# Attention blocks of the third and fourth chunk issued in pairs, with part of their transfers on ScalarE

## The chip, the cores and the metric

The kernel runs on one core of a Trainium2 chip. The metric is the device time of one execution in microseconds; the median of three runs is quoted, with the lowest and the highest.

## What is computed

A windowed attention over 8 batches and 8 heads of 576 positions with 64 columns each, then a feed-forward product over the 4608 tokens that it leaves. Heads 0 to 3 see the last 32 positions; heads 4 to 7 see every fourth of the last 128.

```python
scores = scale * np.matmul(q, k.transpose(0, 1, 3, 2))
rel = pos[:, None] - pos[None, :]
mask_plain = (rel >= 0) & (rel < window)                                          # window = 32
mask_dil = (rel >= 0) & (rel < window * dilation) & (rel % dilation == 0)         # dilation = 4
scores = np.where(masks[None], scores, -1e9)
attn = np.exp(scores - np.max(scores, axis=-1, keepdims=True))
attn = attn / (np.sum(attn, axis=-1, keepdims=True) + 1e-09)
x = np.matmul(attn, v)            # to 4608 tokens of 512
...
h = x @ w_in                      # 512 -> 2048
g = h * np.clip(h + 3.0, 0.0, 6.0) / 6.0
return g @ w_out                  # 2048 -> 512
```

All inputs and the output are fp32.

## The kernel before

**Products in three parts.** A matrix product of fp32 numbers is made of three products on TensorE: each operand is split into a high and a low part (`xh`, `xl`, `gh`, `gl`), and high by high, low by high and high by low are summed in PSUM.

**Tokens and steps.** The 4608 tokens lie in 12 chunks of 384. Chunks 0 to 3 are computed plainly, in steps `m` of one chunk and one block of 128 of the 2048 hidden columns, 16 steps a chunk: steps 32 to 47 are the third chunk, 48 to 63 the fourth. A step is `first(m)` and `second(m - 2)`. `first` is 12 matmuls of 128x384 into a bank of `ps_h` (L483 to L485), then relu on ScalarE (L491), the gate on VectorE (L494), which is the last to read the bank, and the two halves of the gated numbers, `gh` on ScalarE (L498) and `gl` on VectorE (L502). `second` is 9 matmuls of 128x512 into three banks of output (`ps_o`, L533 to L535). The other eight chunks follow with a Strassen scheme of fewer products (`pair`), streaming sums of weights from DRAM.

**PSUM.** Eight banks: two for `ps_h`, six for `ps_a`, of which three hold the output sums of a chunk.

**Attention.** The work is cut into 48 trios `t`. A block `block(ts, tv)` makes the scores of one trio and the values of an earlier one: 24 small matmuls of each kind on tiles of 64x32 of the array (L202, L220), by turns. The trace shows two records for each. Scores go through a chain: the mask is added (L228, VectorE; the reader of the bank), the largest taken (L239), subtracted (L243), the exponential (L249, ScalarE), two transposes by 32x32 blocks on VectorE (L325 into `a_t`, L326 into `a`), and four transfers of 24 KB (L331 to L335, function `cross`) that carry the pieces of `a_t` to the other partitions of `a`. `a` is what the value products of the block two later read. Values are normalised (L254 to L257, the last reader of their bank), transposed, crossed by four transfers in the same way (`xf`), then split into `xh` (L384, ScalarE) and a low part (L390 to L392, GpSimd) that the first product of later chunks reads. The loads of queries and keys (`kq`, L173) and of values (`v`, L182) for the trio two later are issued after the block.

The first 12 trios run with the first chunk, in an order written by hand. Blocks `b` = 0 to 17 (scores of trio 12 + b, values of trio 10 + b) run one by one among the steps of the third and fourth chunk, after `second`, about every 1.9 steps, at the steps that the list `spots` in the last function gives. Blocks from 18 on run inside `pair`.

**Order.** TensorE's instructions run in the order in which the steps are recorded. For VectorE, ScalarE, GpSimd and SyncE a planner sets the order: `op(engine, us, do, after, lag, takes, gives)` records an operation with an estimated duration, what it follows, a lag until its result has landed and the buffers that it takes and gives; `_in_time` lays the recorded operations out in time and gives each engine its list. All DMAs of the kernel before are issued by SyncE. All waits are on semaphores; a DMA also waits for the landing of the eighth DMA before it.

**Beside the blocks.** The same stretch prepares the weights for the Strassen part: sums of weight blocks on VectorE (L559, L567), a high part on ScalarE (L571), a low part (L576), and their stores to DRAM (`sums`, L583 to L590, on SyncE). At the end of a chunk the output is scaled and stored (`out`, L767).

## Time and profile before

| what | before |
|---|---|
| median of 3 runs | 870.23 us (867.68 to 871.71) |
| the profiled execution | 868.87 us |
| its span, first to last instruction | 867.1 us |
| granted TensorE clock, mean | 0.996 |
| DMA bytes moved | 148.30 MB, mean 171 GB/s |
| stretch of the single blocks | about 172 to 335 us |

Times in the profile are microseconds from the start of the span. PE is TensorE's matmul, PEld its weight load, DVE VectorE, ACT ScalarE, POOL GpSimd, SP SyncE; SPq is SyncE's issuing of DMAs. L202 is line 202 of the kernel. A row of a timeline gives start, duration, engine, line, operation, output <- inputs, shape and count, and in brackets the idle time before it with the event that ended it. A row of the windows gives the stretch, its length, then busy time and count of PE, PEld, DVE, ACT and POOL, the granted clock, the share of DMA and GB/s.

### The profile page before, as it was taken

The page shows a single profiled execution, that of the slowest core. Times are in us where ns is not written, and L with a number is a line of the kernel's source. Part 1 is how long each engine was busy: PE and PEld are TensorE (multiplying, and loading weights), DVE is VectorE, ACT ScalarE, POOL GpSimd, SP SyncE. Part 2 cuts the span into 40 slices and gives each one's busy share as a digit, 9 for nine tenths or more (in the row PEclk, how much of TensorE's full clock was granted, in tenths as well). Part 3 has the DMA queues.
Part 4 walks back from the last instruction along what each step waited for, and adds up shares of the span by engine and source line. Part 5 has one row for each costly group of instructions (what it writes and reads, how often), then busy time and mean ns, then how long its engine had stood idle before and what let it go on. Part 6 is the DMA issues. An engine that isn't in the chain of part 4 may idle for free.

```text
span 867.1 us, 20779 instructions
## 1 busy us (share of the span) xinstructions
PE 850.5 (98%) x8540; PEld 754.9 (87%) x8540; DVE 561.6 (65%) x1148; ACT 394.3 (45%) x746; POOL 30.9 (4%) x78
## 2 busy tenths in 40 slices
PE   7899999999999999999999999999999999999998
PEld 4698898888888878888888889888988889989997
DVE  3999986578886777665667565567556457343342
ACT  3788775343333424433436433335543335443334
POOL 0000000000100100100000000000000000000000
PEclk8999999999999999999999999999999999999999
DMA  8756335446677575664544655553654432753001
GB/s 288 278 163 205 122 122 173 155 158 214 206 230 230 150 254 181 208 219 146 210 145 147 224 173 178 180 187 114 226 193 145 145 120 95 277 193 113 1 1 73
DMA packets 83246, 148.30 MB, mean 171 GB/s; under 512 B 9808, under 2 KB 33360, under 8 KB 83152
## 3 DMA queue, kind: packets, MB, share of 16 engines
q1 hardware_dynamic: 83152, 146.98, 51.3%
q8 instruction: 67, 1.10, 0.5%
q14 instruction: 27, 0.22, 0.1%
HBM read 115.74 MB, written 24.12 MB: 161 GB/s over the span
## 4 chain that ended last, share of the span: by engine, by line
PE 91%; DMA 3%; SPq 2%; DVE 2%; ACT 1%; issue 1%; DVEq 0%; ACTq 0%
PE ps_o L643 11%; PE ps_o L645 10%; PE ps_o L644 10%; PE ps_x L653 9%; PE ps_x L655 9%; PE ps_x L654 9%; PE ps_h L483 5%; PE ps_h L485 4%; PE ps_h L484 4%; PE ps_o L533 4%; PE ps_o L535 4%; PE ps_o L534 4%; SPq L333 2%; PE ps_b L220 2%; PE ps_a L202 2%; PE ps_a L220 1%
## 5 line engine op out<-in xcount | busy, mean ns | idle before, releaser
L643 PE MATMUL ps_o<-wo,gh 128*128 128x512 f32 x384 | 152.0, 396 | 0.0
L645 PE MATMUL ps_o<-wo,gl 128*128 128x512 f32 x384 | 150.2, 391 | 0.0
L644 PE MATMUL ps_o<-wo,gh 128*128 128x512 f32 x384 | 150.0, 391 | 0.0
L904 DVE TENSOR_TENSOR s<-ps_x,s 128x384 f32<-128x384 f32 x96 | 53.3, 556 | 121.7 <-ACT s L898 68.8
L653 PE MATMUL ps_x<-xh,ring 128*128 128x384 f32 x384 | 129.5, 337 | 0.0
L898 ACT COPY s<-ps_x 128x384 f32<-128x384 f32 x96 | 46.2, 481 | 182.8 <-PE ps_x L655 177.6
L654 PE MATMUL ps_x<-xl,ring 128*128 128x384 f32 x384 | 129.0, 336 | 0.0
L655 PE MATMUL ps_x<-xh,ring 128*128 128x384 f32 x384 | 129.0, 336 | 0.0
L862 DVE TENSOR_TENSOR gl<-t,gh 128x384 fp32r<-128x384 f32 x128 | 71.8, 561 | 57.1 <-ACT gh L858 53.6
L858 ACT CAST gh<-t 128x384 fp32r<-128x384 f32 x128 | 65.8, 514 | 54.8 <-DVE t L866 53.6
L483 PE MATMUL ps_h<-xh,wi 128*128 128x384 f32 x256 | 88.9, 347 | 0.0
L485 PE MATMUL ps_h<-xh,wi 128*128 128x384 f32 x256 | 86.1, 336 | 0.0
L484 PE MATMUL ps_h<-xl,wi 128*128 128x384 f32 x256 | 86.1, 336 | 0.0
L645 PEld LDWEIGHTS ps_o<-wo,gl 128*128 128x128 f32 x384 | 72.1, 188 | 15.6
L643 PEld LDWEIGHTS ps_o<-wo,gh 128*128 128x128 f32 x384 | 72.1, 188 | 11.6
L644 PEld LDWEIGHTS ps_o<-wo,gh 128*128 128x128 f32 x384 | 72.1, 188 | 10.0
L854 ACT ACTIVATE t<-s,three 128x384 f32<-128x384 f32 x96 | 59.2, 617 | 42.6 <-DVE s L904 42.4
L653 PEld LDWEIGHTS ps_x<-xh,ring 128*128 128x128 f32 x384 | 72.2, 188 | 3.9
L654 PEld LDWEIGHTS ps_x<-xl,ring 128*128 128x128 f32 x384 | 72.2, 188 | 3.9
L533 PE MATMUL ps_o<-wo,gh 128*128 128x512 f32 x192 | 74.9, 390 | 0.0
L534 PE MATMUL ps_o<-wo,gh 128*128 128x512 f32 x192 | 74.7, 389 | 0.0
L535 PE MATMUL ps_o<-wo,gl 128*128 128x512 f32 x192 | 74.7, 389 | 0.0
(96 smaller groups left out, 1447.1 us busy)
## 6 DMA issues: line engine op xcount, KB each, us to landing
ring<-sums SPq DMA_DIRECT2D x112, 512.0 KB, 4.6
st<-in_w SPq DMA_DIRECT2D x32, 512.0 KB, 3.6
kq<-in_qk SPq DMA_DIRECT2D x39, 416.0 KB, 6.2
v<-in_v SPq DMA_DIRECT2D x39, 390.0 KB, 4.2
out<-o SPq DMA_DIRECT2D x36, 256.0 KB, 3.0
sums<-wi SPq DMA_DIRECT2D x24, 256.0 KB, 4.9
sums<-sh SPq DMA_DIRECT2D x8, 512.0 KB, 5.3
sums<-v SPq DMA_DIRECT2D x8, 512.0 KB, 6.8
```

The costliest lines, as they stand in the source:

```text
L483: nc.tensor.matmul(ph, lhsT=wt(f, 0)[:, ks], rhs=a, start=(kt == 0), stop=False)
L484: nc.tensor.matmul(ph, lhsT=wt(f, 0)[:, ks], rhs=b, start=False, stop=False)
L485: ins = nc.tensor.matmul(ph, lhsT=wt(f, 1)[:, ks], rhs=a, start=False, stop=(kt == NK - 1))
L533: nc.tensor.matmul(po[c][tt], lhsT=gh[:, rows], rhs=wt(f, 2), start=first, stop=False)
L534: nc.tensor.matmul(po[c][tt], lhsT=gh[:, rows], rhs=wt(f, 3), start=False, stop=False)
L535: return nc.tensor.matmul(po[c][tt], lhsT=gl[:, rows], rhs=wt(f, 2), start=False, stop=(f == NF - 1))
L643: nc.tensor.matmul(bank, lhsT=gh[:, rows], rhs=wt(f, 2), start=first, stop=False)
L644: nc.tensor.matmul(bank, lhsT=gh[:, rows], rhs=wt(f, 3), start=False, stop=False)
L645: nc.tensor.matmul(bank, lhsT=gl[:, rows], rhs=wt(f, 2), start=False, stop=final)
L653: nc.tensor.matmul(bank, lhsT=tile_[:, 0, ks], rhs=h[:, kt], start=(start and kt == 0), stop=False, skip_group_check=True)
L654: nc.tensor.matmul(bank, lhsT=tile_[:, 0, ks], rhs=l[:, kt], start=False, stop=False, skip_group_check=True)
L655: nc.tensor.matmul(bank, lhsT=tile_[:, 1, ks], rhs=h[:, kt], start=False, stop=(kt == 1), skip_group_check=True)
```

## The change

Blocks 0 to 17 become nine pairs, at steps 30, 34, 40, 43, 46, 50, 53, 57 and 60 (`SPOTS`), each after `second`. The two blocks of a pair follow each other on TensorE. Of a pair's four results the first scores go to a bank of `ps_h` (named `ps_b`), the other three to `ps_a`. `cross` becomes four operations of one transfer each. For trios below 30 and `a`, these are issued alternately by ScalarE and SyncE; the four of `xf` stay on SyncE, and so does every transfer of later trios. The waits for `ps_h` banks are now kept in one list of readers, and the planner's accounting of work buffers follows.

```diff
--- before.py
+++ after.py
@@ -37,6 +37,7 @@
 SOON = 4.0
 EVER = 1.0e6
 SLACK = 0.4
+SPOTS = (30, 1), (34, 1), (40, 1), (43, 1), (46, 1), (50, 1), (53, 1), (57, 1), (60, 1)
 
 
 
@@ -267,11 +268,11 @@
     def blocks():
         return [(i, u, r) for i in range(SLOTS) for u in range(2) for r in range(2)]
 
-    def block(ts, tv, pool=None):
-
-        bank = lambda: pool.tile([P, 512], F32, name="ps_b", tag="ps_h") if pool else ps_a.tile([P, 512], F32, name="ps_a")
-        ps = bank() if ts is not None else None
-        pv = bank() if tv is not None else None
+    def block(ts, tv, pools=()):
+
+        bank = lambda pool=ps_a: pool.tile([P, 512], F32, name="ps_b", tag="ps_h") if pool is ps_h else ps_a.tile([P, 512], F32, name="ps_a")
+        ps = bank(*pools[:1]) if ts is not None else None
+        pv = bank(*pools[1:]) if tv is not None else None
         masked = ts is not None and ts < NFIRST
         if masked:
             _, kind, part = trios[ts]
@@ -326,13 +327,12 @@
         nc.vector.transpose(out=dst.rearrange("p (u i y) -> p u i y", u=2, y=QB), in_=twice)
         return dst, mid
 
-    def cross(dst, mid):
-
-        for c in range(4):
-            u, to = c % 2, c ^ 1
-            nc.sync.dma_start(
-                out=dst[QB * to : QB * (to + 1), u * CH // 2 : (u + 1) * CH // 2], in_=mid[QB * c : QB * (c + 1), : CH // 2]
-            )
+    def cross_one(dst, mid, c, queue):
+
+        u, to = c % 2, c ^ 1
+        queue.dma_start(
+            out=dst[QB * to : QB * (to + 1), u * CH // 2 : (u + 1) * CH // 2], in_=mid[QB * c : QB * (c + 1), : CH // 2]
+        )
 
     raws = {}
 
@@ -697,6 +697,9 @@
     raw_seen, stored, freed = set(), [], []
     readers = {"ps_h": [], "ps_a": []}
 
+    def by_two(t):
+        return t < NFIRST + 2 * len(SPOTS)
+
     def turn_over(t, src, into, name, after):
         two = []
 
@@ -705,44 +708,59 @@
             into[t] = two[0]
 
         x = op("DVE", 0.92, do, [after], takes=TWO, gives=ONE, ahead=EVER)
-        return op("SP", 2.6, lambda: cross(*two), [x], lag=3.5, gives=ONE, ahead=EVER)
-
-    def attend(b, pool=None):
-
-        ts = NFIRST + b if NFIRST + b < T else None
-        tv = NFIRST + b - 2 if b >= 2 else None
-        count = (ts is not None) + (tv is not None)
-        bank = "ps_h" if pool else "ps_a"
+        queues = ("SP",) * 4 if name == "xf" or not by_two(t) else ("ACT", "SP") * 2
+        return [
+            op(e, 0.65, lambda c=c, e=e: cross_one(*two, c, nc.sync if e == "SP" else nc.scalar), [x], lag=2.9, gives=ONE if c == 3 and len(set(queues)) == 1 else (), ahead=EVER)
+            for c, e in enumerate(queues)
+        ]
+
+    def attend(bs, pools):
+
+        scores = [NFIRST + b for b in bs if NFIRST + b < T]
+        values = [NFIRST + b - 2 for b in bs if b >= 2]
+        couples = [(NFIRST + b, NFIRST + b - 2) for b in bs]
+        order = [t for x in couples for t in x if t in scores + values]
+        bank, room = dict(zip(order, pools)), {}
+
+        def do():
+            for x in couples:
+                block(*(t if t in bank else None for t in x), [bank.get(t) for t in x])
+
+        names = {x: "ps_h" if bank[x] is ps_h else "ps_a" for x in order}
+        for x in names.values():
+            room[x] = room.get(x, 0) + 1
         beat = op(
-            "PE", 1.42 if count == 2 else 0.8, lambda: block(ts, tv, pool),
-            [turned.get(tv), landed_k.get(ts), landed_v.get(tv), *readers[bank], *(() if pool else stored)],
-            takes=[(bank, count)], gives=ONE if tv is not None else (),
-        )
-        readers[bank] = []
-        stored.clear()
-        if ts is not None:
-            x = op("DVE", 0.55, lambda: add_mask(ts), [beat], takes=ONE, gives=[(bank, 1)], ahead=EVER)
-            readers[bank].append(x)
-            x = op("DVE", 0.55, lambda: largest(ts), [x], ahead=EVER)
-            x = op("DVE", 0.57, lambda: shifted(ts), [x], ahead=EVER)
-            x = op("ACT", 0.53, lambda: exponent(ts), [x], ahead=EVER)
+            "PE", 0.35 + 0.535 * len(order), do,
+            [*(x for t in values for x in turned[t]), *(landed_k.get(t) for t in scores), *(landed_v.get(t) for t in values),
+             *(readers["ps_a"] + stored if "ps_a" in room else ()), *readers["ps_h"][-2:][: room.get("ps_h", 0)]],
+            takes=list(room.items()), gives=[("work", sum(1 + by_two(t) for t in values))],
+        )
+        if "ps_a" in room:
+            readers["ps_a"] = []
+            stored.clear()
+        for ts in scores:
+            x = op("DVE", 0.55, lambda ts=ts: add_mask(ts), [beat], takes=ONE, gives=[(names[ts], 1)], ahead=EVER)
+            readers[names[ts]].append(x)
+            x = op("DVE", 0.55, lambda ts=ts: largest(ts), [x], ahead=EVER)
+            x = op("DVE", 0.57, lambda ts=ts: shifted(ts), [x], ahead=EVER)
+            x = op("ACT", 0.53, lambda ts=ts: exponent(ts), [x], ahead=EVER)
             turned[ts] = turn_over(ts, es, ats, "a", x)
             if ts + NLOAD < T:
-                landed_k[ts + NLOAD] = op("SP", 0.4, lambda: load_qk(ts + NLOAD), [beat], lag=5.0, ahead=EVER)
-        if tv is not None:
-            x = op("DVE", 0.9, lambda: normalise(tv), [beat], takes=ONE, gives=[(bank, 1)], ahead=EVER)
-            readers[bank].append(x)
+                landed_k[ts + NLOAD] = op("SP", 0.4, lambda ts=ts: load_qk(ts + NLOAD), [beat], lag=5.0, ahead=EVER)
+        for tv in values:
+            x = op("DVE", 0.9, lambda tv=tv: normalise(tv), [beat], takes=ONE, gives=[(names[tv], 1)], ahead=EVER)
+            readers[names[tv]].append(x)
             x = turn_over(tv, xs, xfs, "xf", x)
             if tv + NLOAD < T:
-                landed_v[tv + NLOAD] = op("SP", 0.4, lambda: load_v(tv + NLOAD), [beat], lag=5.0, ahead=EVER)
+                landed_v[tv + NLOAD] = op("SP", 0.4, lambda tv=tv: load_v(tv + NLOAD), [beat], lag=5.0, ahead=EVER)
             pieces = [(n, token // CH) for _, n, _, _, token in spans(tv)]
             touched = {c for n, c in pieces if c >= PLAIN} - {c for c, kind in raw_seen if kind == trios[tv][1]}
             raw_seen.update((c, trios[tv][1]) for c in touched)
             plain = [n for n, c in pieces if c < PLAIN]
             if plain:
-                x = op("ACT", sum(0.15 + n / 500 for n in plain), lambda: high(tv), [x], ahead=EVER)
+                x = [op("ACT", sum(0.15 + n / 500 for n in plain), lambda tv=tv: high(tv), x, ahead=EVER)]
             split[tv] = op(
-                "POOL", sum(0.25 + n / 250 for n, _ in pieces), lambda: low(tv, nc.gpsimd), [x], takes=[("w", len(touched), 1)], gives=ONE, ahead=EVER
+                "POOL", sum(0.25 + n / 250 for n, _ in pieces), lambda tv=tv: low(tv, nc.gpsimd), x, takes=[("w", len(touched), 1)], gives=ONE, ahead=EVER
             )
 
     def put_out(c, tt, bank, r, after, parts, last):
@@ -770,9 +788,10 @@
 
     def first(n, after):
         c, f = steps[n]
-        g = op("PE", 12 * 0.173, lambda: gemm1(n), [*after, gated_h.get(n - 2)], takes=[("ps_h", 1)], gives=SLOT if c == PLAIN - 1 else ())
+        g = op("PE", 12 * 0.173, lambda: gemm1(n), [*after, *readers["ps_h"][-2:-1]], takes=[("ps_h", 1)], gives=SLOT if c == PLAIN - 1 else ())
         r = op("ACT", 0.58, lambda: relu(n), [g], takes=ONE)
         t = gated_h[n] = op("DVE", 0.55, lambda: gate(n), [r], gives=[("ps_h", 1)])
+        readers["ps_h"].append(t)
         gh = op("ACT", 0.52, lambda: gate_high(n), [t], takes=ONE)
         gates[n] = gh, op("DVE", 0.58, lambda: gate_low(n), [gh], takes=ONE, gives=ONE)
         return g
@@ -905,9 +924,9 @@
             )
 
         FREE = [("ps_h", 1)]
-        p1 = product(A11, "x", True, readers["ps_h"][:1])
+        p1 = product(A11, "x", True, readers["ps_h"][-2:-1])
         s1 = keep("s1", p1)
-        p2 = product(A12, "y", True, readers["ps_h"][1:])
+        p2 = product(A12, "y", True, readers["ps_h"][-1:])
         c11 = add("s1", "y", [s1, p2], FREE)
         gated(lambda: kept["s1"], c11, g, fa, 0, False)
         run_units(3 if k == 0 else 1)
@@ -952,34 +971,30 @@
 
         free = {"work": WORK, "w": SLOTS_W - 2 * NF, "ps_h": 2, "ps_a": 0}
         free["work"] -= 2 * sum(m not in done for m in range(n))
-        BLOCKS = 18
-        ended_at = [(c + 1) * NF + LAG - 1 for c in range(1, PLAIN)]
-        spots = [NF * 2 - 2 + round(1.9 * b) for b in range(BLOCKS)]
-        spots = [m + (m in ended_at) for m in spots]
         ends_of, firsts, b = {}, {}, 0
         for m in range(n, len(steps)):
             c, f = steps[m]
             g = first(m, [split[t] for t in split if c in chunks(*trios[t])] if f == 0 and c == PLAIN - 1 else ())
             firsts[m] = ends_of[c] = g
-            if m - LAG not in done:
-                second(m - LAG)
-            while b < BLOCKS and spots[b] <= m:
-                attend(b)
-                b += 1
+            for late in range(2):
+                if (m, late) in SPOTS:
+                    attend((b, b + 1), (ps_h, ps_a, ps_a, ps_a))
+                    b += 2
+                if not late and m - LAG not in done:
+                    second(m - LAG)
         for k in range(NF // 2):
             combined[k] = combine(k, [firsts[min(34 + 4 * k, len(steps) - 1)]])
         for at in range(RING):
             bring(at)
         spare = {0: ends_of[PLAIN - 1], 1: ends_of[1], 2: ends_of[2]}
         fill(0, {A11: spare[1], A12: spare[1], S2: spare[2], S1: spare[2], S3: None, A22: spare[0], S4: spare[0]})
-        readers["ps_h"] = [gated_h[len(steps) - 2], gated_h[len(steps) - 1]]
         freed[:] = [None, *readers["ps_a"][-2:]]
         units += [lambda m=m, tt=tt: old_unit(m, tt) for m in range(len(steps) - LAG, len(steps)) for tt in range(TT)]
         for g in range(GROUPS):
             for k in range(NF // 2):
                 now = []
                 if k != NF // 2 - 2 and b < T - NFIRST + 2:
-                    now, b = [lambda b=b: attend(b, ps_h)], b + 1
+                    now, b = [lambda b=b: attend((b,), (ps_h, ps_h))], b + 1
                 pair(g, k, now)
             if g + 1 < GROUPS:
                 fill(g + 1, dict(used))
```

In the new kernel the lines of the blocks stand one lower (L202 is L203, L220 is L221, L228 is L229, and so on to L327; L333 is the transfer again), and the output's transfer is L785.

TensorE, at the end of an ordinary block of before (the second to have values): `kq` are scores, `v,a` values, L483 starts the next first product.

```order
L220 MATMUL ps_a<-v,a 32x65
L202 MATMUL ps_a<-kq 32x64
L220 MATMUL ps_a<-v,a 32x65
L202 MATMUL ps_a<-kq 32x64
L483 MATMUL ps_h<-xh,wi 128x384
L484 MATMUL ps_h<-xl,wi 128x384
```

TensorE, in the middle of the second pair of the changed kernel, where the first block ends and the second begins.

```order
L203 MATMUL ps_b<-kq 32x64
L221 MATMUL ps_a<-v,a 32x65
L203 MATMUL ps_b<-kq 32x64
L221 MATMUL ps_a<-v,a 32x65
L203 MATMUL ps_a<-kq 32x64
L221 MATMUL ps_a<-v,a 32x65
```

The large matmul that followed a block now follows two.

VectorE before, at the end of the third chunk, near 275 us of the trace: a block's mask (L228) to its transposes (L325, L326), with two sums of weights (L559) among them.

```order
L228 TENSOR_TENSOR e<-ps_a,mi 128x384
L254 TENSOR_SCALAR z<-ps_a 128x6
L255 RECIPROCAL z<-z 128x6
L257 TENSOR_TENSOR x<-ps_a,z 128x384
L239 TENSOR_REDUCE mx<-e 128x6
L559 TENSOR_TENSOR v<-wi 128x512
L243 TENSOR_TENSOR e<-e,mx 128x384
L494 SCALAR_TENSOR_TENSOR t<-t,ps_h 128x384
L559 TENSOR_TENSOR v<-wi 128x512
L325 STREAM_TRANSPOSE a_t<-e 128x192
L326 STREAM_TRANSPOSE a<-e 128x384
```

VectorE in the changed kernel behind the sixth pair, which stands at the same end of a chunk: its last normalisation and what follows.

```order
L258 TENSOR_TENSOR x<-ps_a,z 128x384
L559 TENSOR_TENSOR v<-wi 128x512
L494 SCALAR_TENSOR_TENSOR t<-t,ps_h 128x384
L567 TENSOR_TENSOR v<-v 128x256
L559 TENSOR_TENSOR v<-wi 128x512
L502 TENSOR_TENSOR gl<-t,gh 128x384
```

The second L559 here is the one that waits for an output's transfer to free its buffer; masks, maxima, shifts and transposes of both blocks stand ahead of these rows.

ScalarE in the changed kernel around the fourth pair (step 43): the exponentials of the two blocks and the transfers that ScalarE issues, two for each block.

```order
L250 ACTIVATE e<-e 128x384 x2
L498 CAST gh<-t 128x384
L333 DMA a<-a_t 32x192 x4
L491 ACTIVATE t<-ps_h,three 128x384
L498 CAST gh<-t 128x384
L491 ACTIVATE t<-ps_h,three 128x384
```

Before, ScalarE issues no transfer; here four stand ahead of the relu (L491) of a later step.

## The prediction

> **What bounds the kernel now.** First the page: its head, the busy shares and the strip of granted clock.
>
> ```profile
> span 867.1 us, 20779 instructions
> PE 850.5 (98%) x8540; PEld 754.9 (87%) x8540; DVE 561.6 (65%) x1148; ACT 394.3 (45%) x746; POOL 30.9 (4%) x78
> PEclk8999999999999999999999999999999999999999
> ```
>
> TensorE is busy for 98% of the span at full clock. What a change can save is therefore PE work, or the 16.6 us in which PE is not busy. So the second view is the windows by stage; the third column pair is PE, and clock, DMA share and GB/s end a row.
>
> ```profile
> 75.00:172.00 97.00, 97.00 (x490) 87.97 (x489) 76.52 (x142) 61.00 (x113) 0.00 (x0) 1.00 0.46 149
> 172.00:335.00 163.00, 160.64 (x2325) 141.77 (x2324) 129.23 (x283) 59.65 (x109) 11.24 (x24) 1.00 0.64 203
> 350.00:860.00 510.00, 510.00 (x4238) 456.79 (x4224) 285.31 (x567) 211.11 (x400) 18.60 (x47) 1.00 0.46 153
> ```
>
> Between 75 and 172 us and from 350 on, PE never idles. The stretch from 172 to 335 us, where the third and fourth chunk run with the 18 blocks that the change regroups, holds idle PE time. VectorE is busy for 79% of it (129.23 of 163), ScalarE for 37% (59.65). So the third view is PE's timeline around one ordinary block, and around the two longest.
>
> ```profile
> 200.35 0.39 PE L534 MATMUL ps_o<-wo,gh 128*128 128x512 f32 x1
> 200.58 0.39 PE L535 MATMUL ps_o<-wo,gl 128*128 128x512 f32 x1
> 200.90 0.24 PE L220 MATMUL ps_a<-v,a 64*32 64x65 f32 x1
> ...
> 201.86 0.22 PE L202 MATMUL ps_a<-kq 64*32 64x64 f32 x1
> 202.00 0.44 PE L483 MATMUL ps_h<-xh,wi 128*128 128x384 f32 x1
> 202.28 0.34 PE L484 MATMUL ps_h<-xl,wi 128*128 128x384 f32 x1
> 202.46 0.34 PE L485 MATMUL ps_h<-xh,wi 128*128 128x384 f32 x1
> ...
> 282.86 0.39 PE L535 MATMUL ps_o<-wo,gl 128*128 128x512 f32 x1
> 284.00 0.30 PE L220 MATMUL ps_a<-v,a 64*32 64x65 f32 x2 [0.75 <-DMA a<-a_t]
> 285.69 0.44 PE L483 MATMUL ps_h<-xh,wi 128*128 128x384 f32 x1
> ...
> 308.99 0.39 PE L535 MATMUL ps_o<-wo,gl 128*128 128x512 f32 x1
> 310.30 0.24 PE L220 MATMUL ps_a<-v,a 64*32 64x65 f32 x1 [0.92 <-DMA a<-a_t]
> 312.60 0.45 PE L483 MATMUL ps_h<-xh,wi 128*128 128x384 f32 x1
> ```
>
> An ordinary block takes 1.42 us from the start of the last L535 to the start of the next L483 (200.58 to 202.00). The block at 284.00 takes 2.83 by the same measure, the one at 310.30 takes 3.61: they lose 1.41 and 2.19 us, **3.60 together**. Both wait for `a`, the transposed exponentials, whose four transfers bring pieces across partitions. The chain of waits says why these were late.
>
> ```profile
> 270.33 3.97 DMA out<-o
> 275.02 0.69 DVE v L559
> 278.06 5.89 DMA a<-a_t
> ...
> 306.40 0.59 SPq L333
> 307.67 1.42 SPq L333
> 309.76 1.79 DMA a<-a_t
> ```
>
> The rows of SyncE's queue around the second:
>
> ```profile
> 302.29 4.70 SPq L333 DMA_DIRECT2D xf<-xf_t  x4
> 307.09 3.27 SPq L333 DMA_DIRECT2D a<-a_t  x4
> ```
>
> The first time VectorE sat at L559, a sum of weights whose buffer was still held by an output's transfer, with the softmax of the block behind it. The second time SyncE itself was late: it issued four `xf` transfers, then four of `a`, at 0.59 us each where nothing held them and 1.42 where something did, 4.70 and 3.27 for the four.
>
> **The change, part by part.** *One: fewer switches.* The 18 blocks stay, as nine pairs, and the second block of each pair follows its first without a matrix product between them. In the rows around 200 us, L534 to L535 is 0.227 us, but L535 to the first small product is 0.32 (200.58 to 200.90): the entry costs 0.09. After the last small product, L483 starts 0.14 later and L484 another 0.28 after it, where L484 to L485 is 0.18. Taken together: 1.42 for the block, less the 0.227 that L535 takes of it anyway, plus the 0.11 by which L484 is late, is 1.30 us that a lone block adds. Its small products alone run from 200.90 to 201.86, 0.96, and one more step of some 0.01 joins them to the next block. A joined block adds 0.97, so a pair saves 1.30 − 0.97 = 0.33, and nine pairs **3.0 us**. This can be no more than the entry and the exit (0.34 each pair). It can be as little as nothing if products that go on for two blocks run slower. The nearest row for that is the first block of before, with scores alone:
>
> ```profile
> 172.73 0.87 PE L202 MATMUL ps_a<-kq 64*32 64x64 f32 x48
> 173.54 0.45 PE L483 MATMUL ps_h<-xh,wi 128*128 128x384 f32 x1
> ```
>
> Its 48 records (the trace has two of each small product) start over 0.66 us (0.81 to the next L483 less the exit's 0.14), 14 ns each against 10 for the 96 of the mixed block. 96 at that pace take 1.32, and the saving is gone. I take 10 ns, because the second block is mixed like the first, in other banks.
>
> *Two: the two stalls.* In the changed order the L559 ahead of the sixth pair's masks waits for a product only, and the one that needs an output's buffer stands behind both blocks' transposes and normalisations. The 3.60 us wait that held one block's exponentials thus falls where a gate is the next behind it. SyncE's queue had two causes, the number of issues ahead and what held them. With two of each four `a` transfers on ScalarE, SyncE issues two for a block. Both stalls are counted as gone: **−3.6 us**. What would be late next is the pair three steps later. A step is 12 matrix products at 0.174 and 9 at 0.227:
>
> ```profile
> L483 PE MATMUL ps_h<-xh,wi 128*128 128x384 f32 x256 | 88.9, 347 | 0.0
> L533 PE MATMUL ps_o<-wo,gh 128*128 128x512 f32 x192 | 74.9, 390 | 0.0
> L228 DVE TENSOR_TENSOR e<-ps_a,mi 128x384 f32<-128x384 f32 x18 | 9.9, 552 | 2.9 <-PE ps_a L202 2.6
> L239 DVE TENSOR_REDUCE mx<-e 128x6 f32<-128x384 f32 x36 | 19.6, 544 | 0.0
> L249 ACT ACTIVATE e<-e 128x384 f32<-128x384 f32 x48 | 25.1, 527 | 20.8 <-DVE e L243 20.7
> L325 DVE STREAM_TRANSPOSE a_t<-e 128x192 f32<-128x192 f32 x36 | 13.3, 369 | 3.4 <-ACT e L249 2.7 <-DMA xf<-xf_t 0.7
> a<-a_t SPq DMA_DIRECT2D x144, 24.0 KB, 2.1
> ```
>
> (These means overlap in the pipelines; the starts of L533, L534 and L535 give 0.227, those of L484 and L485 0.174.) A step is 12 × 0.174 + 9 × 0.227 = 4.13 us, three are 12.4. From the pair's end both masks, maxima and shifts take 6 × 0.55 = 3.3 us on VectorE, less about 0.5 that the first mask overlaps the second block; then an exponent of 0.53, a gate and the two transposes of each block (0.37 and 0.54) bring the last `a_t` to 5 to 6 us. Four issues on each queue of 0.59 run behind them to 7.5 or 8; they land 2.1 later, at 10. The first use is at 12.4, the second block's a microsecond later: 2 to 3 us to spare. Four of the eight gaps between pairs are of three steps, and in two, before the fifth and the ninth pair, SyncE has more ahead (three `wi` stores, or seven `xf`): at 0.59 each, seven take 4.1 and the last `a` lands at 10; at the 1.18 of the slow case they take 8.2, and it lands at 8.2 + 3.3 + 1.8 = 13.3, about 1 us late. I put **+0.5** for the two, of bounds 0 and 2.
>
> *Three: issues on ScalarE.* 36 transfers move from SyncE to ScalarE, 36 × 0.59 = 21 us more of ScalarE's sequencer against the 163 us of a stretch in which it is 37% busy. Four stand in a pair's steps ahead of the relu two steps on, in order. They cost nothing as long as that relu and its gate are done before the next pair takes the same bank; the rival below prices what happens otherwise.
>
> *Four: banks and the rest.* One of the pair's four results takes a bank of the first product's two. The next product but one needs it back after one mask, at 0.5 us, and starts 4.1 later: nothing, with a bound of 0.5 us once if the mask waits behind VectorE's other work. The last pair runs two steps earlier than the last block did; what follows it has the cover of PE's unbroken 510 us, so it is costed at nothing; if that cover failed it would cost the wait of a later block, below 1 us by the ordinary blocks' spread (1.42 to 1.56).
>
> *Sum:* the profiled execution of before took 868.87 us (span 867.1 and 1.8 around it); −3.0 − 3.6 + 0.5 = −6.1 gives 862.8. It lies 1.36 below the median of the runs shown (870.23), from which the sum would be 864.1. I say **863.4**, between them. A difference of under 0.5% (4.35 us) is about what a measurement of this kernel can't tell from none.
>
> **Rivals.** *A: landings, not issues, set when `a` comes.* The chain's last piece at 309.76 is a landing of 1.79, and the one at 278.06 is told as 5.89 of transfer. Then 96 KB for each of two blocks come at once, with two `kq` and two `v` just before them:
>
> ```profile
> kq<-in_qk SPq DMA_DIRECT2D x39, 416.0 KB, 6.2
> v<-in_v SPq DMA_DIRECT2D x39, 390.0 KB, 4.2
> ```
>
> Their landings put an `a` at 8 + 6.2 = 14.2 where it shares their engines, 1.8 late, in two of the four short gaps: the 3.6 us come back. −3.0 + 0.5 remain, 866.4, or 867.7 from the median. Against it: the median `a` lands in 2.1. [...]
>
> *B: the joined block gets no cheaper* (the 14 ns bound above, or the lead comes back as a wait on `v` or `kq`): −3.6 + 0.5, 865.8. Against it, the mixed block's steady 10 ns.
>
> *C, the slower side: ScalarE held in order.* The `a` transfers wait on ScalarE for the transposes of the second block and, each, for the landing of a transfer eight before it. At 1.42 each, as SyncE's slowest was, four that start at 6 end at 11.7; the relu behind them (0.58) and the gate (0.55) make 12.8 and the pair's bank is late by 0.4; with one landing of a large load (6.2) in the way it is 3.5 more. The point is 11.1 us after a pair. At all four short gaps 3.5 us are 14: 868.87 − 6.1 + 14 = 876.8. For it speaks SyncE's own 4.70 us for four issues; against it, that ScalarE has no large loads of its own.
>
> **How the numbers follow.** Forecast 0.55, A 0.25, B 0.11, C 0.09. Forecast lies over 0.5% faster, A and B within, C slower: 0.55, 0.36, 0.09. Range: below, all 3.6 and 3.0 and no new wait, with the runs' spread of 2 us, 860.5; above, A from the median with 1 us of new waits more, 869.0. That leaves out C and a little on each side.
>
> **What would show it.** Right: in the stretch of pairs PE starts 192 small records about 2.3 us after the last L535 entered, with no L483 between; no block waits more than 0.5 us for `a`; eight of nine pairs at 2.27 us plus entry and exit. Wrong: L220 again waiting for `a` by over 1 us (A), small records at 14 ns (B), L228 or the pair's first product waiting for a gate with ScalarE's relu behind L333 (C), or idle PE after 350 us.

## The result, and the profile after

| | before | changed |
|---|---|---|
| median of 14 runs each | 869.35 us (867.40 to 871.71) | 873.55 us (870.69 to 877.85) |
| the profiled execution | 868.87 us | 872.03 us |
| its span | 867.1 us | 870.2 us |

The changed kernel is **slower**: the ratio is 1.005, with a 95% interval of 1.0035 to 1.0064. The forecast was 863.4 us with a range of 860.5 to 869.0; the time lies outside it, and on the other side of the kernel before.

The page of the changed kernel begins like that of before, with the same work on TensorE.

```profile
span 870.2 us, 20814 instructions
PE 850.8 (98%) x8540; PEld 758.1 (87%) x8540; DVE 559.8 (64%) x1148; ACT 393.9 (45%) x746; POOL 33.0 (4%) x78
```

The windows of the changed kernel, in the stretch of the pairs (the columns as before).

```profile
172.00:335.00 163.00, 155.65 (x2309) 139.88 (x2308) 123.76 (x272) 57.61 (x106) 12.98 (x24) 0.99 0.62 204
```

PE was busy for 160.64 of these 163 us before; now it is 155.65. The loss is idle PE time in the very stretch that the change touches. To measure it free of what precedes and follows, take the time from the first small product of the first block to the first product of the Strassen part (L653). Timelines of PE, first the kernel before (its first small product, at 172.73, is shown in the prediction), then the changed one:

```profile
336.06 0.34 PE L653 MATMUL ps_x<-xh,ring 128*128 128x384 f32 x1
```

```profile
172.46 0.26 PE L203 MATMUL ps_b<-kq 64*32 64x64 f32 x4
...
338.78 0.34 PE L653 MATMUL ps_x<-xh,ring 128*128 128x384 f32 x1
```

The stretch takes 163.33 us before and 166.32 after, 3.0 more, which is nearly all of the 3.1 by which the spans differ. From that product to the start of TensorE's last one both kernels take 526.8 us. Below, "stretch" is always this measure, taken from the profiled execution; it leaves out the start-up, which varies: in the kernels without added products the first block starts anywhere from 170.8 to 175.1 us.

Where the time went is in the list of what PE waited for in 172 to 352 us of the changed kernel (total, times, longest).

```profile
PE ps_b L203 <- DVE t L494: 3.6, 2, 2.6
PE ps_a L221 <- issue: 1.7, 1, 1.7
PE ps_h L484 <- issue: 1.3, 1, 1.3
PE ps_h L485 <- issue: 0.5, 1, 0.5
PE ps_a L221 <- DMA a<-a_t: 0.2, 1, 0.2
```

The two waits of before for `a` are gone (0.2 us is left). New are waits for a gate, L494, and waits put down to "issue", for which the profile shows no releaser. PE's timeline shows the three kinds of pair: the third, undisturbed; the second, of which only the hole in the step behind it is shown; the seventh; and once more an undisturbed one, the eighth.

```profile
218.91 0.39 PE L535 MATMUL ps_o<-wo,gl 128*128 128x512 f32 x1
219.23 0.24 PE L221 MATMUL ps_a<-v,a 64*32 64x65 f32 x1
...
221.31 0.44 PE L483 MATMUL ps_h<-xh,wi 128*128 128x384 f32 x1
...
192.83 0.44 PE L483 MATMUL ps_h<-xh,wi 128*128 128x384 f32 x1
...
193.46 0.34 PE L483 MATMUL ps_h<-xh,wi 128*128 128x384 f32 x1
195.07 0.34 PE L484 MATMUL ps_h<-xl,wi 128*128 128x384 f32 x1 [1.27 <-issue]
...
283.21 0.39 PE L535 MATMUL ps_o<-wo,gl 128*128 128x512 f32 x1
285.32 0.27 PE L221 MATMUL ps_a<-v,a 64*32 64x65 f32 x2 [1.73 <-issue]
288.20 0.31 PE L203 MATMUL ps_b<-kq 64*32 64x64 f32 x1 [2.61 <-DVE t L494]
...
290.93 0.44 PE L483 MATMUL ps_h<-xh,wi 128*128 128x384 f32 x1
...
307.33 0.39 PE L535 MATMUL ps_o<-wo,gl 128*128 128x512 f32 x1
...
309.71 0.44 PE L483 MATMUL ps_h<-xh,wi 128*128 128x384 f32 x1
...
330.05 0.34 PE L484 MATMUL ps_h<-xl,wi 128*128 128x384 f32 x1
330.88 0.34 PE L485 MATMUL ps_h<-xh,wi 128*128 128x384 f32 x1 [0.49 <-issue]
```

An undisturbed pair (the eighth, 307.33 to 309.71) takes 2.38 us from the last L535 to the next L483. The seventh takes 7.72. The holes behind 193.46 and, after the ninth pair, behind 330.05 are of another sort: they lie among the large products of a step, and the profile shows nothing that L484 or L485 would wait for there.

The chain of waits of the changed kernel ahead of the seventh pair, and what ScalarE and SyncE did meanwhile (ACTq and SPq are DMA issues):

```profile
278.81 6.42 DMA v<-in_v
285.25 1.73 DMA a<-a_t
286.98 0.58 ACT t L491
287.59 0.57 DVE t L494
288.20 0.31 PE ps_b L203
```

```profile
277.68 9.12 ACTq L333 DMA_DIRECT2D a<-a_t  x4
286.98 0.58 ACT L491 ACTIVATE t<-ps_h,three 128x384 f32<-128x384 f32 x1 [9.53 <-DMA a<-a_t]
```

```profile
270.19 2.29 SPq L785 DMA_DIRECT2D out<-o  x2
272.56 2.42 SPq L333 DMA_DIRECT2D xf<-xf_t  x4
...
276.25 2.51 SPq L174 DMA_DIRECT2D kq<-in_qk  x2
278.81 0.99 SPq L183 DMA_DIRECT2D v<-in_v  x2
279.90 5.86 SPq L333 DMA_DIRECT2D a<-a_t  x4
```

The sixth pair ended at 270.95. The loads that follow it come out of SyncE's queue only at 276.25 to 279.80, behind an output, four `xf` and two stores of weight sums. The values land at 285.23, and the seventh pair's first product, which reads them, starts at 285.32: that is its wait put down to "issue". Two of ScalarE's four transfers stand on the semaphores of such loads, each eight DMAs before it: the third is issued at 284.11, when a `kq` has landed at 283.95, the fourth at 286.28, when a `v` has landed at 286.26. So four issues take 9.12 us; the relu behind them starts 9.53 us after ScalarE's last work, its gate ends at 288.2, and the pair's bank comes free then.

### The profile page after: what moved, and what is told of

Read it like the earlier page. It is cut to its first block, busy times and chain, and to the rows that moved or that the text cites. A ratio compares the mean times of both kernels' runs of the same rounds, so it can differ in the third digit from the quotient of the medians.

```text
span 870.2 us, 20814 instructions
## 1 busy us (share of the span) xinstructions
PE 850.8 (98%) x8540; PEld 758.1 (87%) x8540; DVE 559.8 (64%) x1148; ACT 393.9 (45%) x746; POOL 33.0 (4%) x78
## 4 chain that ended last, share of the span: by engine, by line
PE 90%; DMA 4%; DVE 2%; SPq 1%; ACT 1%; issue 1%; DVEq 0%; ACTq 0%
PE ps_o L643 11%; PE ps_o L645 10%; PE ps_o L644 10%; PE ps_x L653 9%; PE ps_x L655 9%; PE ps_x L654 9%; PE ps_h L483 5%; PE ps_h L484 4%; PE ps_h L485 4%; PE ps_o L533 4%; PE ps_o L535 4%; PE ps_o L534 4%; PE ps_b L221 2%; PE ps_b L203 1%; DMA a<-a_t 1%; PE ps_a L203 1%
## 5 line engine op out<-in xcount | busy, mean ns | idle before, releaser
L645 PE MATMUL ps_o<-wo,gl 128*128 128x512 f32 x384 | 150.2, 391 | 0.0
L653 PE MATMUL ps_x<-xh,ring 128*128 128x384 f32 x384 | 129.5, 337 | 0.0
L483 PE MATMUL ps_h<-xh,wi 128*128 128x384 f32 x256 | 88.3, 345 | 0.0
L484 PE MATMUL ps_h<-xl,wi 128*128 128x384 f32 x256 | 86.4, 338 | 1.3 <-issue 1.3
L485 PE MATMUL ps_h<-xh,wi 128*128 128x384 f32 x256 | 86.3, 337 | 0.5 <-issue 0.5
L491 ACT ACTIVATE t<-ps_h,three 128x384 f32<-128x384 f32 x64 | 36.9, 580 | 99.4 <-PE ps_h L485 65.0
L653 PEld LDWEIGHTS ps_x<-xh,ring 128*128 128x128 f32 x384 | 72.2, 188 | 3.9
```

The costliest lines, as they stand in the source:

```text
L483: nc.tensor.matmul(ph, lhsT=wt(f, 0)[:, ks], rhs=a, start=(kt == 0), stop=False)
L484: nc.tensor.matmul(ph, lhsT=wt(f, 0)[:, ks], rhs=b, start=False, stop=False)
L485: ins = nc.tensor.matmul(ph, lhsT=wt(f, 1)[:, ks], rhs=a, start=False, stop=(kt == NK - 1))
L645: nc.tensor.matmul(bank, lhsT=gl[:, rows], rhs=wt(f, 2), start=False, stop=final)
L653: nc.tensor.matmul(bank, lhsT=tile_[:, 0, ks], rhs=h[:, kt], start=(start and kt == 0), stop=False, skip_group_check=True)
```

## The experiments

Three theories. **H**: ScalarE is held by the transfers that it issues (9.12 us for the four above, with the relu behind them), and makes relu and gate late; in a second form, whatever is issued behind late loads, on either queue, waits for their landing. **R**: a pair simply needs its `a` too early. **F**: TensorE waits for its own instructions.

F came from the trace's records of the DMA queue of instructions (q8 of the changed kernel's page): 67 fetches of 16384 bytes. PE's records (weight loads, matmuls, semaphore events), counted from the start, give 17292 in all. That is 67.5 times 256, so F estimates 256 instructions to a fetch, 64 bytes each; the instructions of one fetch are called a line here. Both holes that need no data end at a count of 256 x n + 193, and 1.49 and 1.43 us after a fetch landed.

```
hole ends    count     count mod 256    last fetch landed
195.07       4545      193              193.58
330.88       8385      193              329.45
```

A block of 96 small records, each with its weight load, is 192 instructions, a pair 384. With lines that start at 256 x n + 193, no fetch in the stretch of the changed kernel or of the one before starts earlier than 292 instructions ahead of the line that it brings, 36 ahead of the start of the line before. Counted from that point, the 36 fetches of the two stretches start from 0.2 us before it to 7.6 us behind it (lower quartile 1.1, median 1.4, upper quartile 2.3 us behind) and take 0.9 to 1.7 us, 1.1 in the median. The two holes end 3.9 and 6.6 us behind it; the shortest time in which PE reached a line without a hole of over 0.4 us is 4.16 us. From these F estimates 1 to 1.4 us until a fetch starts, 1 us for the fetch and 1.4 to 1.5 us until it is used: 3.5 to 4 us in all. The estimate is rough. The 192 products of the eighth pair, 384 instructions, start over 1.92 us, 5.0 ns each, so a line inside a burst is used up in 1.3 us by this estimate. By F a pair should stall where its place against the lines puts most of a line inside it, and a single block nowhere. That place can be computed for any order of the steps (a step is 42 instructions).

**All transfers by SyncE.** The new pairs, with the old queue.

```diff
-        queues = ("SP",) * 4 if name == "xf" or not by_two(t) else ("ACT", "SP") * 2
+        queues = ("SP",) * 4
```

> The nine pairs of the changed kernel, all transfers of a issued by SyncE again. Theory H (ScalarE, held in order by the transfers that it issues, makes relu and gate late): no wait of a pair for a gate (L494) is left. The seventh pair loses at most the 2 us of its wait for values instead of 5.3, the ninth nothing instead of 1.2, the fourth and fifth nothing instead of 1.4; SyncE's later issues give back up to 1. About 868.5 us, 4 to 6 under the changed kernel. Theory F (TensorE waits for its own instructions after a burst of two blocks): the same gap of about 1.4 us in the step after the second pair, since TensorE's order is the same. Rival R (a pair needs its a too early, whoever issues it): L221 waits for a at the pairs three steps after another, in sum 3 us or more, and the time stays at 873 or goes up.

Measured: 877.33 us, ratio to before 1.0083 (1.0058 to 1.0108); stretch 171.67. The waits of PE:

```profile
PE ps_a L221 <- DMA a<-a_t: 5.3, 5, 2.4
PE ps_a L221 <- issue: 1.7, 1, 1.7
PE ps_h L484 <- issue: 1.3, 1, 1.3
PE ps_b L203 <- DVE t L494: 0.7, 1, 0.7
```

The waits for gates are nearly gone, but 5.3 us for `a` come instead: R's result, and H's time is missed by 9 us. The division of the queues **helps** the pairs (by 3.8 us in the medians, 5.4 in the stretch); the pairs alone are what costs. The hole of 1.3 us behind the second pair stays, as F says; another of 1.7 us, which F had not named, stands in the fifth, at count 193 of 256 again.

**Single blocks with divided transfers.**

```diff
-SPOTS = (30, 1), (34, 1), (40, 1), ...
+SPOTS = tuple((m + (m in (33, 49)), 1) for m in (30 + round(1.9 * b) for b in range(18)))
...
-                    attend((b, b + 1), (ps_h, ps_a, ps_a, ps_a))
-                    b += 2
+                    attend((b,), (ps_a, ps_a))
+                    b += 1
```

> The 18 single blocks of before at their old steps, with the new kernel's division of the transfers between ScalarE and SyncE. H: some of the gates come late here too, but a block issues only two transfers on ScalarE and has 3.8 steps to its use: 0 to 2 us of waits for gates, and the 3.6 us of two waits for a may go or stay; 866 to 871. F: no gap in the steps after a block, as in before, since a single block is half as many instructions. R: no loss, up to 4 us faster than before.

Measured: 867.96 us, ratio 0.9979 (0.9955 to 1.0003); stretch 160.19, 3.1 below before. PE waits for nothing in the whole stretch:

```profile
172.00:335.00 163.00, 163.00 (x2340) 144.43 (x2339) 130.54 (x287) 61.57 (x113) 12.24 (x24) 1.00 0.67 209
```

In the stretch the second half of the change is worth what the two stalls of before cost, when it is made without the first. In the medians it is 2.0 us, with an interval that still includes no change.

**Pairs every four steps**, with transfers divided, and with all of them on SyncE.

```diff
-SPOTS = (30, 1), (34, 1), (40, 1), (43, 1), (46, 1), (50, 1), (53, 1), (57, 1), (60, 1)
+SPOTS = tuple((30 + 4 * i, 1) for i in range(9))
```

> Pairs at steps 30, 34, 38 and so on to 62, four steps apart throughout, transfers divided as in the changed kernel. H alone: 4.1 us more room at the four short gaps, so that the 5.3 us wait falls to about 1: near 863.7. F: the stalls depend on where a burst lies against the 256 instructions of one fetch. By counting instructions from the changed kernel's trace, the second, third, fourth, eighth and ninth pair lie so that one whole fetch of 256 is used up inside the burst: gaps of 1.4, 2.2, 2.2, 1.5 and 2.2 us, 9.5 together, and none at the fifth, sixth and seventh; about 873. R: as H, near 863.

> Pairs four steps apart, all transfers of a by SyncE. H alone: no wait for a gate, near 862.5. F: the same five gaps of 9.5 us in sum, about 872. R: near 863, with a waited for if SyncE is late.

Measured: 881.75 us (ratio 1.0125, 1.0076 to 1.0174; stretch 175.59) and 881.54 us (1.0139, 1.0081 to 1.0196; stretch 176.15). The holes lie at the five pairs that F named, and at no other; excess over the usual spacing, in us:

```
pair                      2      3      4      8      9     sum
expected                 1.4    2.2    2.2    1.5    2.2    9.5
divided                  1.16   2.86   3.46   0.96   2.58  11.0
all on SyncE             1.72   3.29   2.61   2.02   3.93  13.6
```

Each ends at count 193 or 194 of 256, and 1.3 to 1.6 us after a fetch landed. H alone and R, which asked for 863, fall by 18 us; yet their part holds where F leaves the pairs alone: the seventh pair, now four steps after the sixth, waits for nothing. H's wait has not gone altogether: behind the eighth pair of the divided run a step waits 1.8 us for a gate, whose relu started 8.6 us after ScalarE's last work, behind its transfers. Two holes of the divided run cost more than their length. Windows of that run, in the hole of the fourth pair, behind it, and later (the third number from the end is the granted clock):

```profile
236.30:239.80 3.50, 0.29 (x27) 0.15 (x16) 0.89 (x2) 0.07 (x1) 2.18 (x6) 1.00 1.01 313
239.80:243.60 3.80, 3.75 (x51) 3.66 (x51) 1.94 (x4) 0.00 (x0) 0.00 (x0) 0.67 0.63 201
244.00:248.00 4.00, 4.00 (x21) 3.57 (x20) 3.14 (x9) 2.03 (x4) 0.00 (x0) 0.94 0.35 116
```

Over the 3.8 us behind the hole the granted clock is 0.67 in the mean. Behind the third pair's hole it is 0.66 from 216.3 to 219.0 us, and large products start 0.32 us apart there (217.18 to 220.05) instead of 0.174. This doesn't follow every hole, and not by its length alone. The first row is behind a hole of 2.61 us (the fourth pair with all on SyncE), the second behind one of 1.86 us (the fifth pair of pairs_all_sp):

```profile
238.30:242.30 4.00, 4.00 (x57) 3.71 (x57) 2.32 (x5) 0.99 (x2) 0.00 (x0) 1.00 0.84 250
254.90:258.10 3.20, 3.20 (x12) 3.20 (x11) 1.73 (x4) 0.23 (x1) 1.16 (x3) 0.50 0.94 302
```

What decides it isn't shown here.

**The second pair 18 instructions earlier.**

```diff
-SPOTS = (30, 1), (34, 1), (40, 1), ...
+SPOTS = (30, 1), (34, 0), (40, 1), ...
```

> The changed kernel with its second pair before second of step 34 instead of after it, 9 large products earlier, so that 18 fewer instructions lie ahead of the pair. F: a burst loses nothing where its trigger or its end lies outside the two blocks; the second pair's line of 256 then ends some 27 instructions behind the burst instead of 9, about 2 us later, and the gap of 1.4 us in the step after it is gone. Everything behind stands as before against the lines. About 1.4 us less than the changed kernel, 872; no other gap moves. H: nothing changes, 873.5.

Measured: 868.2 us, ratio 0.999 (0.9974 to 1.0006). The hole behind the second pair is gone; the small one behind the ninth, which F expected to stay, shrank from 0.65 to 0.21 us. The time fell by 5.3 us where 1.4 was expected. The profiled executions don't show why: their stretches are 166.04 and 166.32, and the seventh pair's waits are the same in both (2.08 and 2.83 beyond the usual spacing, against 1.80 and 2.81); this profiled execution, at 871.22, is the slowest of its ten. What the other executions gained more stays open.

**Only the sixth pair's transfers on SyncE.**

```diff
-        return t < NFIRST + 2 * len(SPOTS)
+        return t < NFIRST + 2 * len(SPOTS) and t not in (22, 23)
```

> The changed kernel with the eight transfers of the sixth pair's a back on SyncE, no other transfer moved. H: the relu behind them on ScalarE no longer waits for the landing of a load of values; the seventh pair's wait for the gate, 2.8 us, is gone, its wait for values and a, 1.8 us, stays or grows by up to 1.2: 1.5 to 2.8 us less than the changed kernel, 871. F alone: no change, and the gap of 1.4 us after the second pair stays, as TensorE's order is the same. R: SyncE's eight issues make a later and the time goes up.

Measured: 875.12 us, ratio 1.0055 (1.0033 to 1.0077); stretch 167.50. The seventh pair's wait for the gate is gone, as H says, and PE waits 2.6 us for `a` there instead (2.65 beyond the usual spacing). The gain of 1.5 to 2.8 us that H expected didn't come: the median is 1.6 us above the changed kernel's, as R expected. So the gate was late through ScalarE's queue, but freeing it gains nothing, since the loads and transfers that both queues wait for are late themselves. Another wait of 2 us for `a` appears at the ninth pair, and waits for gates of 1.1 and 1.6 us at the fifth and the ninth.

**The lines shifted.** 64 tiny products on zeros, ahead of everything; all else as in the changed kernel.

```diff
+    for _ in range(64):
+        nc.tensor.matmul(idle[:, :16], lhsT=zeros[:, :P], rhs=zeros[:, P : P + 16], start=True, stop=True)
```

> The changed kernel with 64 tiny products on zeros ahead of everything, 128 more instructions on TensorE at a time when it waits for its first data; the order of all else is the same. F: every pair now lies 128 instructions further against the lines of 256. The second pair comes free (its gap goes), the third to fifth lie as the second did (1.4 us each), the sixth to ninth with a whole line inside the burst (2.2 to 3.5 us each, as the four-step pairs showed), and a second after each longer gap TensorE runs at 0.66 of its clock, 1.3 us more each: 12 to 20 us more in all, partly in place of the waits there now, 882 to 892. H or R alone: no more than the 1 to 2 us that the products themselves may cost, under 876.

Measured: 891.46 us, ratio 1.0272 (1.0233 to 1.0311); stretch 174.34, 8.0 above the changed kernel's. The rest of the difference is start-up: the first block of this run starts at 182.12 instead of 172.46. PE's waits, all of them without a releaser:

```profile
PE ps_a L205 <- issue: 6.5, 2, 4.3
PE ps_a L223 <- issue: 4.2, 2, 2.2
PE ps_h L486 <- issue: 1.3, 2, 0.7
PE ps_h L487 <- issue: 1.0, 1, 1.0
```

The second pair is free; the third, fourth and fifth lose 1.15, 0.77 and 0.89 us beyond the usual spacing, the sixth to ninth 2.44, 2.18, 2.34 and 4.53, all at count 193 or 194. The same instructions in the same order stall elsewhere, where the count says. The waits for gates disappear, presumably because PE now comes later than the gates.

**The control: the kernel before with the same 64 products.**

```diff
+    for _ in range(64):
+        nc.tensor.matmul(idle[:, :16], lhsT=zeros[:, :P], rhs=zeros[:, P : P + 16], start=True, stop=True)
```

> The kernel before with the same 64 tiny products on zeros ahead of everything. F: a single block is 192 instructions, so no line of 256 is used up inside it wherever it lies; no gap, and the time stays within 1 us of before (869.6), against 18 more for the pairs. If the products themselves, or a shift as such, cost the time of lines_shifted, 880 or more.

Measured: 876.04 us, ratio 1.008 (1.0054 to 1.0105). The time missed the expectation by 6 us, and the start accounts for it: the first block starts at 180.07 instead of 172.73. The stretch is 163.02 us against 163.33, with no hole, and its only waits are for `a`, as in before. So single blocks lost nothing to fetches at either place, and of the 18 us of lines_shifted about 8 belong to the pairs.

**The pairs respaced**, so that no line falls inside one, with the sixth a step later.

```diff
+SPOTS = (30, 1), (34, 0), (40, 1), (43, 1), (47, 1), (51, 1), (54, 1), (57, 1), (60, 1)
```

> Pairs at steps 30, 34 (before second), 40, 43, 47, 51, 54, 57 and 60: the sixth one step later, so that it doesn't follow the chunk's output at once, and all so that no pair holds a whole line of 256 instructions. F and H together: no gap behind a burst; the seventh pair's waits of 4.6 us fall to 1 or less; what remains is 1 to 3 us at the four short gaps. 864 to 868, the first version that would beat the kernel before by what the pairs save. F wrong: gaps elsewhere, no gain over 872. H wrong: the same wait at one of the short gaps, 870 or more.

Measured: 871.12 us, ratio 1.0021 (1.0001 to 1.0041); stretch 164.95. The 864 to 868 expected were missed. No hole, as F says; but the seventh pair, three steps after the sixth again, waits 2.5 us for its gate, and the ninth for a gate and for `a`.

**The loads by ScalarE**, once with all `a` on SyncE, once with `a` divided as well.

```diff
-                landed_v[tv + NLOAD] = op("SP", 0.4, lambda tv=tv: load_v(tv + NLOAD), [beat], lag=5.0, ahead=EVER)
+                landed_v[tv + NLOAD] = op(*(("ACT", 0.6, lambda tv=tv: load_v(tv + NLOAD, nc.scalar)) if by_two(tv + 2) else ...
```

> Second pair before second of step 34 as in second_pair_earlier; all transfers of a on SyncE; instead ScalarE issues the loads of queries, keys and values that follow a pair. H in its second form (the seventh pair waits because the loads that follow the sixth are issued 8 us late on SyncE, behind an output, and whatever is issued behind them, on either queue, waits for their landing): these loads go out within 3 us of the pair's end, the values land 6 us later, ahead of the seventh pair; its 4.9 us of waits fall to 1 or less; 862 to 866. R (SyncE's eight transfers of a per pair are too many in three steps): waits for a of 2 to 3 us at one or two short gaps as in the runs with all a on SyncE; 868 to 875. F: no gap behind the second pair.

> As loads_on_scalar, but the transfers of a divided between ScalarE and SyncE as in the changed kernel, so that ScalarE issues eight DMAs a pair. H in its first form (what ScalarE issues holds its relu): waits for gates of 2 to 5 us at several pairs, since its four transfers now follow four large loads on the same queue; 868 to 876. H in its second form: the loads are early, so 862 to 868.

Measured: 885.29 us (ratio 1.0193, 1.0159 to 1.0227; stretch 178.00) and 875.86 us (1.0081, 1.0055 to 1.0107; stretch 166.50). ScalarE's timeline in the first, behind the sixth pair:

```profile
273.29 1.59 ACTq L174 DMA_DIRECT2D kq<-in_qk  x2
277.59 2.70 ACTq L183 DMA_DIRECT2D v<-in_v  x2
280.39 0.58 ACT L491 ACTIVATE t<-ps_h,three 128x384 f32<-128x384 f32 x1 [10.65 <-DMA sums<-sh]
```

The loads didn't go out early: they wait on ScalarE too, for DMAs eight before them (the first goes out at 273.29, 3.5 us after ScalarE's last work, the third at 277.59), and hold the relu for 10.65 us. PE waits 7.8 us for gates in this run. H in its first form is shown again, by making it worse; the hope in its second form, that another queue brings the loads out early, falls here, because the waits go with the order of all DMAs, as those of the changed kernel at 284.11 and 286.28 do, and not with the queue. In the second run the loads do go out sooner, 0 to 5.4 us behind the sixth pair's end instead of 5.3 to 8.9, and the seventh pair's values land 10.7 us behind it instead of 14.3; in this run PE still waits 3.6 us for gates and 2.3 without a releaser, so its time lies where the first form had it and not at the 862 to 868 of the second.

The first run also misses what F expected, no gap behind the second pair:

```profile
192.64 0.34 PE L485 MATMUL ps_h<-xh,wi 128*128 128x384 f32 x1 [0.37 <-issue]
```

This is a hole of 0.53 us at count 193. In the four other runs with the second pair at this place (second_pair_earlier, pairs_respaced, loads_on_scalar_split, pairs_then_singles) the line's fetch landed 1.84 to 2.07 us ahead of its use and nothing stalled; here it started some 1.5 us later against PE's count and landed only 1.40 us ahead. F's count alone missed this hole, where the fetch itself was late.

**Pairs in the third chunk, singles in the fourth.**

```diff
+SPOTS = (30, 1), (34, 0), (40, 1), (43, 1), (46, 1)
+ONES = 50, 51, 53, 55, 57, 58, 60, 62
...
+            if m in ONES:
+                attend((b,), (ps_a, ps_a))
+                b += 1
```

> Five pairs in the third chunk (steps 30, 34 before second, 40, 43, 46), then eight single blocks in the fourth at the steps of before, transfers divided. H and F together: the fourth chunk waits for nothing, as in singles_split; five pairs save 5 x 0.33 = 1.7; the fifth pair loses up to 1: 865 to 868, a little below singles_split (867.96). If the pairs' waits are not from what follows one another in three steps, 870 or more.

Measured: 866.74 us (861.26 to 870.45), ratio 0.9969 (0.9947 to 0.9992); stretch 160.55. No hole; one wait of 1.0 us for `a` is left. Of the 1.7 us that five joins should save nothing shows in the stretch: by the time from the last L535 to the next first product, blocks and pairs lose 3.2 us against undisturbed ones, in singles_split 1.1. It is the fastest version here and beats both kernels; that it beats singles_split, whose stretch is 160.19, isn't shown.

## Why the prediction was wrong

*Fewer switches, −3.0 us.* Right in mechanism and size where nothing disturbs a pair: 2.38 us for the eighth, 2.40 for the third, against the 1.42 + 0.97 = 2.39 of the sum. The bound at which this saving is gone, mixed small records at 14 ns, was met once, in the seventh pair, behind its waits: there the granted clock is 0.53. (The first pair, scores alone, kept the 14 ns that the first blocks of before have.)

```profile
288.20:290.90 2.70, 2.70 (x190) 2.64 (x190) 2.70 (x7) 1.48 (x3) 0.00 (x0) 0.53 0.59 186
```

*The two stalls, −3.6 us.* Right that they go, and singles_split shows it cleanly: its stretch is 3.1 us shorter.

*New waits, +0.5 us, of bounds 0 and 2.* **This term is the first failure.** It measured 6.5: beyond the usual spacing, 4.6 at the seventh pair, 1.2 at the ninth, 0.7 at the fifth. The step that failed is the reckoning that brought the last `a` to 10 us and left "2 to 3 us to spare". It looked for trouble before the fifth and ninth pair, where SyncE has stores or `xf` ahead, and took the pair behind the chunk's output to be safe because VectorE's wait there had moved. But the output still stood in SyncE's queue, ahead of the loads that follow the pair, and these came out 5 to 9 us behind the pair's end. Part three had put ScalarE's issues at nothing on the condition that relu and gate are done before the next pair; that condition failed here. Rival C had the mechanism and nearly the price (3.5 us for one landing of a large load in the way, a figure for which it shows no working), and its point of 11.1 us behind the pair was passed: the last of ScalarE's issues ended at 286.8, 15.8 us after 270.95. It got 0.09 with the reason that ScalarE has no large loads of its own. That reason was wrong: ScalarE's third and fourth issue waited for the DMA eight before each, and SyncE had issued both of those. The third went out at 284.11, after a load had landed at 283.95, the fourth at 286.28, after one had landed at 286.26. C's own sum, 3.5 at all four short gaps, was too high; it happened in full at one.

*What wasn't in it at all.* The 2.1 us of holes behind the second and the ninth pair (1.43 and 0.65). **No step of the prediction asked whether PE gets its instructions as fast as two joined blocks use them.** The page showed the queue of instructions, 67 packets and 1.10 MB, and nothing was made of it. The runs have 24 holes of over 0.4 us at the end of a line, at count 193 or 194, in seven of the eleven kernels with pairs (two in the changed kernel, five in each of the four-step runs, seven in lines_shifted, two in pairs_all_sp and in sixth_pair_sp, one in loads_on_scalar), and none in the three with single blocks alone.

*The sum.* −3.0 for the joins; −3.1 for the waits of before that went, as PE's starts show them; +6.5 and +2.1 make 2.5 of the 3.0 by which the stretch grew. The rest is in blocks that ran slowly without a listed wait. By the prediction's own measure, last L535 to next L483, the pairs lose 8.2 us against 2.39 each (0.7 of it more in the seventh, at the low clock), and the mixed blocks of before lost 4.2 against 1.42 each; −3.0 − 4.2 + 8.2 + 2.1 makes 3.1. The medians differ by 4.2. The range's own working gives 860.3 and 868.7 for its bounds, and C's point comes to 11.3 by its terms; none of this changes the outcome.

*The rivals A and B.* A's 3.6 us came back, though not as landings of `a`: the landing that held things up was a load's. The split alone took both stalls away: singles_split has neither. B didn't happen where the clock was full.

*Parts that held.* Nothing after the stretch changed (526.8 us in both), so the later blocks and the ring were rightly costed at nothing.

## What to carry to other kernels

Joining two bursts of tiny instructions saved one switch here, 0.33 us. But pairs of 384 instructions, against 256 to a fetch by F's estimate, lost 0.5 to 4.5 us at 24 places of seven runs, with a granted clock of 0.66 and 0.67 behind two of them in pairs_every_four, while single blocks of 192 had no such hole; and with 128 more instructions ahead (lines_shifted) other pairs stalled. So count the instructions of a burst before it is made longer, and look where it lies in the program. Here the second engine that issued DMAs shared the waits of the first (its issues of 284.11 and 286.28 followed landings of SyncE's loads), and the relu queued behind them started 9.53 us after ScalarE's last work: look for the slowest transfer a few DMAs ahead in the order of all DMAs, not for what that engine itself issues. Two edits that come together can have opposite signs, here −3.1 us of the stretch for the transfers alone and +8.3 for the pairs alone (171.67 against 163.33); try each alone.

## What the runs showed of the hardware

- TensorE's fetch of instructions: in the stretches of the changed kernel and of the one before, 36 fetches of 16384 bytes took 0.9 to 1.7 us, 1.1 in the median. In the changed kernel's two holes PE went on 1.49 and 1.43 us after one had landed, in the ten of the four-step runs 1.3 to 1.6 us. The 384 instructions of the changed kernel's eighth pair started 5.0 ns apart, 1.92 us in all.
- The granted clock behind holes and waits of PE (lengths beyond the usual spacing): 0.53 from 288.2 to 290.9 us of the changed kernel, behind waits of 1.80 and 2.81 us; in pairs_every_four 0.66 over 2.7 us behind a hole of 2.86 us and 0.67 over 3.8 us behind one of 3.46 us; 0.50 over 3.2 us behind one of 1.86 us in pairs_all_sp; but 1.00 over 4.0 us behind one of 2.61 us in pairs_every_four_sp. Behind the hole of 2.86 us nine large products came 0.15 us late each.
- Four DMA issues took 2.42 us on SyncE in the changed kernel (272.56, `xf`), and 9.12 us on ScalarE (277.68, `a`), where two of them stood until loads of SyncE's had landed.
